# A one-column ordering write moved from VectorE to ScalarE in a fused attention and feed-forward kernel

## The chip, the cores and the metric

The kernel runs on one core of a Trainium2 chip. The core has five engines that run in parallel, each through its own queue in order: TensorE (PE, with its weight loads shown apart as PEld), VectorE (DVE), ScalarE (ACT), GpSimd (POOL) and SyncE (SP, which issues most DMAs). An engine waits for another through semaphores. The metric is the device time in microseconds of one execution, as a median of three runs; lower is better. "Visit 13" below means a turn of the kernel's main loop, explained in the section on the kernel.

## The reference

Attention with normalised queries and keys over 8 batches, 12 heads, 448 positions and a head size of 64, followed by a feed-forward block with SiLU:

```python
def rmsnorm(x, g):
    rms = np.sqrt(np.mean(x * x, axis=-1, keepdims=True) + 1e-06)
    return x / rms * g
q_n, k_n = (rmsnorm(q, g_q), rmsnorm(k, g_k))
scores = scale * np.matmul(q_n, k_n.transpose(0, 1, 3, 2))
attn = np.exp(scores - np.max(scores, axis=-1, keepdims=True))
attn = attn / (np.sum(attn, axis=-1, keepdims=True) + 1e-09)
x = np.matmul(attn, v)               # then (B,H,S,D) -> (B*S, H*D)
h = x @ w_in                         # 3584 x 768 times 768 x 2048
g = h * (1.0 / (1.0 + np.exp(-h)))
out = g @ w_out                      # 2048 x 768
```

All data is fp32.

## The kernel before

The attention part is a loop over 24 visits, `visit(c)` followed by `between(c)`. A visit handles four heads: two pairs `i`, each with two heads `h`. Scores are made with the keys on the partitions, in chunks `j` of 2 x 64 keys; the last, smaller chunk is called `LEFT`. `scores(c, j, i)` (line 590) is four 64x64 matmuls, which fill the four quadrants of the array together and which the trace shows as two groups of four, since each fp32 product takes two passes. ScalarE then takes the exponential of two banks (line 604); its scale is the reciprocal norm of the key rows.

The weighted sums, `weigh(c, j, step)` (line 615), are again 64x64 matmuls. Two PSUM banks, `banks[0]` and `banks[1]` (tile `av`), hold the sums of the two pairs. A matmul reads 64 rows of the array, the upper or the lower half, and which half goes to which bank depends on `step`: in arrangement 0 the half is `i`, in arrangement 1 it is the other one (line 625). So each bank gets sums from both halves over a visit. When the arrangement turns, a matmul of one row half would write a bank which matmuls of the other half may still be writing. Two things keep them in order. `turn(step)` (line 609) writes one unused column of `banks[1]`, column S, from a constant: this write waits for the earlier matmuls into the bank, and the next matmuls into the bank wait for the write. Where the visit is `crowded` (line 1337: those in `visits`, in `sums_visits`, and visits 6, 12 and 18; seven in all) the second turn of the visit makes no write, and `weigh` instead puts a drain into TensorE's queue (line 622), which holds until its earlier matmuls are done. On a turn `weigh` takes bank 1 first.

The order inside a visit is written out by hand (lines 1272 to 1327), and the schedule is manual: each engine's queue holds its instructions in the order of the program text. In a visit the order is: scores (0,0); the squares of the next visit's q (up to visit 6); the last two sums of the visit before in arrangement 0; `turn(1)`; scores (0,1); the last sum in arrangement 1; copies or divisions of the finished sums; scores (1,0) and (1,1); squares of k; sum (0) in arrangement 1; scores (2,0); sum (1) in arrangement 1; `turn(0)`; scores (2,1); sums (0) and (1) in arrangement 0; scores (LEFT). The exponentials of a chunk stand on ScalarE's queue where the scores stand in the text.

The squares (`Norm.squares`, line 398) are a ScalarE activation followed by a VectorE reduction; then come a small VectorE operation (line 430) and a power on GpSimd (line 434). In `before`, `split` (line 1333) runs the two parts of some of these pieces apart: part 0 (the ScalarE square) ahead of the sums and the turn, part 1 (the VectorE reduction and what follows) after the turn. This is done for the first piece of q around `turn(1)` and for the last piece of k around `turn(0)`.

GROUP is 6. In visits 0 to 5 the normalisation of the next visit, the reciprocals of the softmax sums (`invert`, line 680) and the rounding of w_in (`Rounder`, line 55: ScalarE, VectorE and GpSimd) go beside the visits. From visit 6 on, the normalisation is done in `between`, which also fills TensorE with products of the feed-forward's first layer (`fill`, line 1211; class `Seven`), of which the SiLU (line 917) runs on ScalarE. As SiLU and the exponential use different tables of ScalarE, `between` ends with a small exponential (line 1380) that makes the table load happen there. PSUM banks `sc` for the scores are two; transposes of the next q and k use them too. After the loop `visit(24)` does the last sums, and the second layer follows.

Of the kernel before, what the change touches and what calls it, by code (L numbers as in the profile page):

```python
# [12 lines left out]
AF = mybir.ActivationFunctionType  # L13
ALU = mybir.AluOpType
AX = mybir.AxisListType
# [367 lines left out]
class Norm:  # L383
# [11 lines left out]
        n = self.at[0 if j == self.z.KEYS else i][0] + 2 * j + h  # L395
        return self.rms[c % 2][:, n : n + 1]

    def squares(self, rows, t, out, parts=(0, 1)):
        nc, n = self.nc, out.shape[1]
        t = t[0 : rows.shape[0], 0 : rows.shape[1]]  # L400
        if 0 in parts:
            nc.scalar.activation(t, rows, AF.Square)  # L402
        if 1 in parts:
            nc.vector.tensor_reduce(  # L404
                out=out, in_=t.rearrange("p (n d) -> p n d", n=n), axis=AX.X, op=ALU.add
            )

    def squares_q(self, c, rows, t, i, parts=(0, 1)):
        R = self.z.R
        size = self.nq * self.z.D  # L410
        self.squares(rows[0:R, ts(i, size)], t, self.rms[c % 2][0:R, ts(i, self.nq)], parts)

    def squares_k(self, c, rows, t, i, parts=(0, 1)):
        start, n = self.at[i]
        first = (self.z.KA, self.z.KB)[i]
        self.squares(
            rows[:, ds(first, n * self.z.D)], t, self.rms[c % 2][:, ds(start, n)], parts
        )

    def root(self, c, name, i=None):  # L420

# [45 lines left out]
def bounded(  # L467
# [3 lines left out]
    P, D, R, J, S = z.P, z.D, z.R, z.J, z.S  # L471
# [6 lines left out]
    NC, loads, place, norm, spare, ones, first = (  # L478
        own[name] for name in ("NC", "loads", "place", "norm", "spare", "ones", "first")
    )  # L480
    GROUP = z.NPAIR
# [9 lines left out]
    parts = mem.tile([P, 2 * S], F32, name="parts")  # L491
    work = mem.tile([P, 16 * S + z.NK], F32, name="work")
    at = 0

    def piece(n):
        nonlocal at
        at += n
        return work[:, at - n : at]
# [16 lines left out]
    n = 2 * room.COLS  # L515
# [10 lines left out]
    def raw_of(c):  # L526
        return own["second_q"] if c == 1 else raw_q[c % 2]

    def q_of(c):
        return rows_q[c % 2 if c < GROUP else 0]  # L530

    def load_q(c):

        if 0 < c < GROUP:
            loads["q"](c, raw_of(c), True)
        elif GROUP <= c < NC:
            loads["q"](c, q_of(c), False)

    def weights(c, j):

        return other if j == 0 and c < GROUP and c % 2 else e[j]
# [45 lines left out]
    weighed = dict(step=1)  # L587
    banks = [None] * 2

    def scores(c, j, i=None):  # L590


        two = ps.tile([P, 2, BANK], F32, name="sc", bufs=2)
        for half in range(2):
            pair = half if j == LEFT else i
            keys = kT[:, ds((z.KA, z.KB)[0 if j == LEFT else i] + j * P, P)]
            for h in range(2):
                rows = ds(h * D, D)
                nc.tensor.matmul(  # L599
                    two[ds(half * D, D), h, 0:S], keys[rows, ts(half, D)], qT[rows, pair, :],  # L600
                    start=True, stop=True,
                )
        for h in range(2):
            nc.scalar.activation(  # L604
                eleft[:, h] if j == LEFT else weights(c, j)[:, i, h], two[:, h, 0:S], AF.Exp,
                scale=norm.column(c, i, h, j),
            )

    def turn(step, later=False):

        weighed["drain"] = later
        if step != weighed["step"] and not later:
            nc.vector.tensor_copy(banks[1][:, S : S + 1], minus_half)  # L613

    def weigh(c, j, step=0):

        order = (0, 1) if step == weighed["step"] else (1, 0)  # L620
        if step != weighed["step"] and weighed.get("drain"):
            nc.tensor.drain()
        weighed["step"] = step
        for i in order:
            half = i if j == LEFT else (i + step) % 2
            rows = ds(half * D, D)
            if j == 0 and step == 1:
                banks[i] = ps.tile([P, BANK], F32, name=f"av{i}")
                sums[i] = banks[i][:, 0:S]
            for h in range(2):  # L630
                if j == LEFT:
                    v, w = place[f"vleft{c % 2}"][rows, ts(h, D)], eleft[rows, h]
                else:
                    w = weights(c, j)[rows, i, h]
                    if j == LEFT - 1:
                        v = place[f"vlast{c % 2}"][rows, ts(2 * i + h, D)]
                    else:
                        v = place["v"][rows, ds(((2 * i + h) * (LEFT - 1) + j) * D, D)]
                nc.tensor.matmul(  # L639
                    sums[i][ds(h * D, D), :], v, w,  # L640
                    start=(j == 0 and step == 1), stop=(j == LEFT - 1 and step == 1),
                )
# [58 lines left out]
    def normalise(c):  # L701


        if c >= NC:
            return []

        def piece(name, i, parts=(0, 1)):
            t = scratch[i if c < GROUP + 2 else 0]
            source = raw_of(c) if c < GROUP else q_of(c)
            if name == "q":  # L710
                norm.squares_q(c, source, t, i, parts)
            else:
                norm.squares_k(c, place[f"k{c % 2}"], t, i, parts)
            if 1 not in parts:
                return
            if name == "q" and c < GROUP:
                norm.root(c, name, i)
                norm.scale(c, source, q_of(c), i, nc.gpsimd)
                if i == 1 and c + 2 < GROUP:
                    load_q(c + 2)  # L720
            elif i == 1:
                norm.root(c, name)
                if name == "q":
                    for m in range(2):
                        norm.scale(c, source, q_of(c), m, nc.gpsimd)

        return [
            lambda *parts, a=a: piece(*a, *parts)
            for a in (("q", 0), ("q", 1), ("k", 0), ("k", 1))
        ]  # L730


    def minus(a, b, out):
# [257 lines left out]
    size = HF * 2 * P  # L991
# [6 lines left out]
    for at in ((1, 2), (2, 1), (2, 2)):  # L998
        a = take(2 * z.HALF)
        results[at] = [a[:, ts(t, z.HALF)] for t in range(2)]  # L1000
    a = take(2 * z.HALF)
# [250 lines left out]
    visits = {GROUP + 2: "rr", GROUP + 4: "rr"}  # L1252
    sums_halves = {-6: [(0, 0)], -5: [(0, 1)], -4: [(0, 2)], -3: [(0, 3)]}
    sums_halves.update({8: [(3, 0), (3, 1)], 9: [(3, 2), (3, 3)]})
    sums_visits = {GROUP + 1: 1, GROUP + 3: 2}
# [16 lines left out]
    def visit(c):  # L1272

        beside = normalise(c + 1) if c <= GROUP else []
        if c < NC:
            scores(c, 0, 0)
        split(beside[0:1], 0)
        if c > 0:
            weigh(c - 1, LEFT)
            weigh(c - 1, LEFT - 1, 0)  # L1280
            turn(1)
        split(beside[0:1], 1)
        if c < NC:
            scores(c, 0, 1)
        if c == 0:
            run_all(beside[1:2])
        if c > 0:
            weigh(c - 1, LEFT - 1, 1)
            if c - 1 < EARLY:
                for i in range(2):  # L1290
                    nc.vector.tensor_copy(x_of(c - 1, i), sums[i])
                run_all(beside[1:2])
                if inverting:
                    if c > 1:
                        divide(c - 2, None)
                    run_all(inverting)
                    inverting.clear()
            else:
                divide(c - 1, sums)
                run_all(beside[1:2])  # L1300
                if c < NC and c % GROUP == 0:
                    for i in range(0 if c == GROUP else 1, HW):
                        sum_x(last_two(c), i)
                weights_in_visit(c)
            if c + 1 < NC:
                loads["vrest"](c + 1)
        if c == NC:
            return
        scores(c, 1, 0)
        scores(c, 1, 1)  # L1310
        if c < GROUP:
            run_all(beside[2:3])
        weigh(c, 0, 1)
        scores(c, 2, 0)
        if c < GROUP:
            split(beside[3:4], 0)
        weigh(c, 1, 1)
        turn(0, crowded(c))
        if c < GROUP:
            split(beside[3:4], 1)  # L1320
        scores(c, 2, 1)
        weigh(c, 0, 0)
        run_all(add(c, 1))
        weigh(c, 1, 0)
        scores(c, LEFT)
        if c + 1 < NC:
            loads["v"](c + 1)

    def run_all(work):
        for piece in work:  # L1330
            piece()

    def split(work, part):
        for piece in work:
            piece((part,))

    def crowded(c):
        return c in visits or c in sums_visits or (c >= GROUP and c % GROUP == 0)

    def between(c):  # L1340

# [49 lines left out]
    for c in range(NC):  # L1391
        visit(c)
        between(c)
# [9 lines left out]
    for m in range(2):  # L1403
        rows = [staged() for _ in range(2)]
# [215 lines left out]
```

## Time and profile before

| | |
|---|---|
| median of 3 runs | 1348.41 us (1348.09 to 1349.94) |
| profiled execution | 1349.43 us, span of its instructions 1347.6 us |
| granted TensorE clock, mean | 0.997 |
| VectorE idle before the column write, for TensorE | 57.5 us, 27 times |
| exponentials (line 604), 324 of 128x448 | 634 ns each |
| sums (line 639), 1296 matmuls of 64x64 by 448 | 547 ns each, four at a time |
| scores (line 599), 1344 matmuls of 64x64 by 448 | 547 ns each, four at a time |
| ScalarE table load of line 1380, 17 times | 1283 ns each |
| visits 0 to 6 | about 0 to 140 us |
| visits 7 to 23 | about 140 to 757 us |
| second layer and rest | from about 765 us |

The span counts from the first to the last instruction of the profiled execution; the execution's own time is 1.8 us longer. A group of four 64x64 matmuls overlaps with the next one, so that the starts of the groups, and not the length of one matmul, show how fast TensorE goes. Of an instruction that waits, the time line shows in brackets how long its engine was idle before it and which instruction released it.

### The profile page before, as it was taken

Reading aid. Unit: us, or ns where it says so; the run is one execution under the profiler, and the core shown is the slowest. Engines: PE = TensorE matmul, PEld = TensorE weight load, DVE = VectorE, ACT = ScalarE, POOL = GpSimd, SP = SyncE. Lnnn points to the kernel's source line nnn. Section 1 sums busy time; section 2 is a strip of 40 time slices with the busy share of each in tenths; the row PEclk is TensorE's granted clock in tenths of the full one; section 3 lists DMA queues with packets and bytes.
Section 4 is the critical chain, followed back from the end, with each engine's and each line's share of the span. In section 5 each row is a group of like instructions: output and inputs, shape, how many; then the busy total and the mean of one; then the engine's idle time right before and its main releaser. Section 6 shows DMA issues by size and latency. Waiting matters only on the chain.

```text
span 1347.6 us, 19775 instructions
## 1 busy us (share of the span) xinstructions
PE 1315.5 (98%) x7345; PEld 841.3 (62%) x7345; DVE 925.6 (69%) x1634; ACT 515.5 (38%) x884; POOL 343.1 (25%) x241
## 2 busy tenths in 40 slices
PE   8898999999999999999999999999999999999998
PEld 4333444444444444444444455557999999999997
DVE  5687877785655544644544587679878787878785
ACT  7766565655455555545544244320000010101000
POOL 6564534343233332333221044420000000000001
PEclk9999999999999999999999999999999999999999
DMA  9554435333223223222311257521323232322321
GB/s 245 146 143 120 121 111 161 99 99 81 78 76 102 79 78 100 76 75 79 104 54 38 100 171 255 160 98 57 116 74 99 75 98 81 98 89 91 111 62 39
DMA packets 175422, 139.42 MB, mean 103 GB/s; under 512 B 104052, under 2 KB 159284, under 8 KB 175316
## 3 DMA queue, kind: packets, MB, share of 16 engines
q1 hardware_dynamic: 174640, 137.08, 34.5%
q8 instruction: 60, 0.98, 0.3%
q0 software_dynamic: 352, 0.79, 0.2%
q14 instruction: 46, 0.38, 0.1%
q10 hardware_dynamic: 324, 0.20, 0.1%
HBM read 88.47 MB, written 41.29 MB: 96 GB/s over the span
## 4 chain that ended last, share of the span: by engine, by line
PE 84%; DVE 5%; ACT 5%; issue 2%; DMA 2%; SPq 1%; POOL 1%; ACTq 0%; DVEq 0%; POOLq 0%
PE mm L779 27%; PE alone L1086 22%; PE mm L1086 7%; PE alone L779 7%; PE av L639 7%; PE sc L599 7%; PE alone L1123 2%; PE sc L562 1%; ACT work L604 1%; PE sc L580 1%; DVE work L682 1%; PE sc L673 1%; DMA work<-work 1%; PE mm L1123 1%; ACT L1380 1%
## 5 line engine op out<-in xcount | busy, mean ns | idle before, releaser
L779 PE MATMUL mm<-x,W 128*128 128x448 f32 x636 | 253.9, 543 | 3.1 <-DVE stage L737 1.2
L604 ACT ACTIVATE work<-sc,rms 128x448 f32<-128x448 f32 x324 | 184.3, 634 | 83.6 <-PE sc L599 67.1
L434 POOL TENSOR_TENSOR rms<-rms,minus_half 128x14 f32<-128x14 f32 (+4 forms) x55 | 137.9, 2509 | 237.5 <-DVE rms L430 169.2
L779 PEld LDWEIGHTS mm<-x,W 128*128 128x128 f32 x636 | 117.8, 190 | 125.0 <-issue 107.1
L779 PE MATMUL mm<-sums_x,W 128*128 128x448 f32 x456 | 183.0, 542 | 1.2 <-DVE parts L737 1.2
L599 PE MATMUL sc<-work 64*64 64x448 f32 x1344 | 165.1, 547 | 3.1 <-ACT work L604 2.6
L639 PE MATMUL av<-work,rows 64*64 64x448 f32 x1296 | 153.8, 547 | 8.6 <-DVE av L613 7.2
L779 PEld LDWEIGHTS mm<-sums_x,W 128*128 128x128 f32 x456 | 85.3, 190 | 86.9 <-issue 80.8
L653 DVE TENSOR_TENSOR work<-work 128x896 f32<-128x896 f32 (+1 forms) x114 | 124.6, 1126 | 19.7 <-PE av L639 15.1
L461 POOL DMA_DIRECT2D out_dram<-x x4 | 2.3, 566 | 442.9 <-DVE x L737 442.8
L639 PEld LDWEIGHTS av<-work,rows 64*64 64x64 f32 x1296 | 56.1, 133 | 84.1 <-issue 44.3
L599 PEld LDWEIGHTS sc<-work 64*64 64x64 f32 x1344 | 52.0, 133 | 86.5 <-ACT work L604 34.4
L404 DVE TENSOR_REDUCE rms<-squares 112x8 f32<-112x512 f32 (+1 forms) x80 | 52.3, 654 | 64.7 <-ACT squares L402 63.9
L1086 PE MATMUL alone<-W,rows 128*128 128x192 f32 x488 | 92.1, 326 | 0.0
L799 POOL TENSOR_TENSOR parts<-parts,stage 128x448 f32<-128x448 f32 x31 | 42.1, 1357 | 157.5 <-DVE parts L737 157.2
L1086 PEld LDWEIGHTS alone<-W,rows 128*128 128x128 f32 x488 | 81.5, 190 | 0.0
L1086 PE MATMUL alone<-W,work 128*128 128x192 f32 x382 | 72.2, 326 | 0.0
L917 ACT ACTIVATE stage<-stage 128x896 f32<-128x896 f32 x63 | 57.3, 945 | 26.1 <-DVE stage L737 25.4
L1086 PEld LDWEIGHTS alone<-W,work 128*128 128x128 f32 x382 | 63.8, 190 | 0.0
L682 DVE RECIPROCAL work<-sc 128x224 f32<-128x224 f32 x36 | 55.7, 1548 | 11.1 <-PE sc L673 11.1
L1096 ACT COPY squares<-alone 128x192 f32<-128x192 f32 x34 | 10.8, 317 | 137.0 <-PE alone L1086 78.4
L402 ACT ACTIVATE squares<-rows 128x512 f32<-128x512 f32 (+1 forms) x74 | 44.8, 605 | 47.5 <-DVE rms L404 46.0
(249 smaller groups left out, 2124.9 us busy)
## 6 DMA issues: line engine op xcount, KB each, us to landing
hidden<-stage SPq DMA_DIRECT2D x63, 448.0 KB, 2.7
work<-hidden SPq DMA_DIRECT2D x21, 1024.0 KB, 5.0
rows<-in_moe_w_out_dram SPq DMA_DIRECT2D x32, 384.0 KB, 3.4
W<-in_moe_w_in_dram SPq DMA_DIRECT2D x22, 512.0 KB, 5.1
rows<-in_k_dram SPq DMA_DIRECT2D x48, 192.0 KB, 3.2
work<-work SPq DMA_DIRECT2D x144, 56.0 KB, 1.9
rows<-in_q_dram SPq DMA_DIRECT2D x36, 224.0 KB, 3.5
x<-hidden SPq DMA_DIRECT2D x7, 1024.0 KB, 5.7
```

The source lines that it names most:

```text
L402: nc.scalar.activation(t, rows, AF.Square)
L404: nc.vector.tensor_reduce(out=out, in_=t.rearrange("p (n d) -> p n d", n=n), axis=AX.X, op=ALU.add)
L434: nc.gpsimd.tensor_tensor(out=t, in0=t, in1=half, op=ALU.pow)
L599: nc.tensor.matmul(two[ds(half * D, D), h, 0:S], keys[rows, ts(half, D)], qT[rows, pair, :], start=True, stop=True,)
L604: nc.scalar.activation(eleft[:, h] if j == LEFT else weights(c, j)[:, i, h], two[:, h, 0:S], AF.Exp, scale=norm.column(c, i, h, j),)
L639: nc.tensor.matmul(sums[i][ds(h * D, D), :], v, w, start=(j == 0 and step == 1), stop=(j == LEFT - 1 and step == 1),)
L653: nc.vector.tensor_tensor(out=total, in0=total, in1=more, op=ALU.add)
L682: nc.vector.reciprocal(out=r[0][:, rows], in_=t[:, rows])
L779: nc.tensor.matmul(t, self.left(name, s), self.right(name, s), start=s == ends[0], stop=s == ends[1])
L799: nc.gpsimd.tensor_tensor(out=u2, in0=u2, in1=p5, op=ALU.add)
L917: nc.scalar.activation(t, t, AF.Silu)
L1086: nc.tensor.matmul(t, x[:, i], y, start=i == ORDER[0], stop=i == ORDER[-1])
```

## The change

Every turn is now a one-column write by ScalarE; VectorE's writes and the drains are gone, and with them `crowded`. The pieces of squares are no longer split: the first piece of q is issued whole ahead of the sums (its ScalarE square stood there before; its VectorE reduction, the small operation and GpSimd's power and scaling now stand there too), and the last piece of k is issued whole after `turn(0)`, so that its ScalarE square now comes behind the column write, where it came ahead of the sum before.

```diff
-    def turn(step, later=False):
-
-        weighed["drain"] = later
-        if step != weighed["step"] and not later:
-            nc.vector.tensor_copy(banks[1][:, S : S + 1], minus_half)
+    def turn(step):
+
+        if step != weighed["step"]:
+            nc.scalar.copy(banks[1][:, S : S + 1], minus_half)
...
         order = (0, 1) if step == weighed["step"] else (1, 0)
-        if step != weighed["step"] and weighed.get("drain"):
-            nc.tensor.drain()
         weighed["step"] = step
...
         if c < NC:
             scores(c, 0, 0)
-        split(beside[0:1], 0)
+        run_all(beside[0:1])
         if c > 0:
             weigh(c - 1, LEFT)
             weigh(c - 1, LEFT - 1, 0)
             turn(1)
-        split(beside[0:1], 1)
         if c < NC:
             scores(c, 0, 1)
...
         weigh(c, 0, 1)
         scores(c, 2, 0)
+        weigh(c, 1, 1)
+        turn(0)
         if c < GROUP:
-            split(beside[3:4], 0)
-        weigh(c, 1, 1)
-        turn(0, crowded(c))
-        if c < GROUP:
-            split(beside[3:4], 1)
+            run_all(beside[3:4])
         scores(c, 2, 1)
         weigh(c, 0, 0)
         run_all(add(c, 1))
...
-    def split(work, part):
-        for piece in work:
-            piece((part,))
-
-    def crowded(c):
-        return c in visits or c in sums_visits or (c >= GROUP and c % GROUP == 0)
-
```

The rest of the diff removes the `parts` argument from `squares`, `squares_q`, `squares_k` and `normalise`.

## The prediction

> **What bounds the kernel now.** I read the page first (busy shares, slices), then the instructions of the column write and of the drain by source line, then the time line around every one of these 48 places.
>
> ```profile
> PE 1315.5 (98%) x7345; PEld 841.3 (62%) x7345; DVE 925.6 (69%) x1634; ACT 515.5 (38%) x884; POOL 343.1 (25%) x241
> ...
> DVE  5687877785655544644544587679878787878785
> ACT  7766565655455555545544244320000010101000
> ```
>
> TensorE is the bound: 98% busy, so a change is worth what it does to the places where TensorE waits. ScalarE is busy 50 to 70% in the first eight slices (visits 0 to 6, up to some 135 us) and about half after.
>
> ```profile
> L613 DVE COPY av<-minus_half x41: 143/161/164, 17.7 to 761.2; 128x1 f32<-128x1 f32 x41
> ...
>   PEld av L639: 28.7, 41
> ...
>   PE av L639: 10.7, 7
> ```
>
> ```profile
> L622 PEldq DRAIN  x7: 1727/1750/2623, 135.4 to 554.5; - x7
> ```
>
> 41 column writes of 0.16 us on VectorE, and 7 drains. In the waiters' list only 7 column writes hold matmuls up; the rest are done while TensorE still works on the scores in between. The drain's 1.75 us is time in which TensorE works its queue off; what it costs is read from matmul starts. In the steady state a group of four 64x64 matmuls starts every 0.375 us. In visit 7 the last scores group before the drain starts at 173.37 with its last matmul at 173.67, and the next starts at 174.35: about 0.6 us lost. In visit 12 it is 0.3 (345.31 to 346.00, less 0.375).
>
> The largest wait is in visit 2 (time line; start, length, engine, line):
>
> ```profile
> 50.97 1.20 PE L599 MATMUL sc<-work 64*64 64x448 f32 x8
> 51.32 2.96 DVE L682 RECIPROCAL work<-mm 128x224 f32<-128x224 f32 x2
> ...
> 54.20 0.62 DVE L404 TENSOR_REDUCE rms<-squares 128x8 f32<-128x512 f32 x1
> 54.74 0.14 DVE L613 COPY av<-minus_half 128x1 f32<-128x1 f32 x1
> ...
> 54.94 3.23 PE L639 MATMUL av<-work,rows 64*64 64x448 f32 x16 [2.77 <-DVE av L613]
> ...
> 59.27 0.63 ACT L604 ACTIVATE work<-sc,rms 128x448 f32<-128x448 f32 x1 [5.85 <-PE sc L599]
> ```
>
> ```profile
> 40.00:60.00 20.00, 17.23 (x155) 7.17 (x151) 14.74 (x26) 13.53 (x25) 11.40 (x8) 0.91 0.58 170
> ...
> 80.00:100.00 20.00, 20.00 (x167) 8.91 (x169) 17.06 (x27) 16.26 (x29) 12.81 (x8) 1.00 0.61 153
> ```
>
> VectorE is in two reciprocals and a reduction, the column write is queued behind them, and TensorE stands still for 2.77 us. After that 16 matmuls take 3.23 us where 1.7 is usual: the granted clock of that window is 0.91, not 1.00. Then ScalarE has been idle 5.85 us. Visit 3 repeats this (gap 2.75 us before 75.05); visit 1 has 0.84 us before 36.52.
>
> The opposite picture is in the middle, visit 13:
>
> ```profile
> 374.84 0.16 DVE L613 COPY av<-minus_half 128x1 f32<-128x1 f32 x1 [0.42 <-PE av L639]
> 374.91 4.45 ACT L604 ACTIVATE work<-sc,rms 128x448 f32<-128x448 f32 x8
> ...
> 376.11 2.03 PE L599 MATMUL sc<-work 64*64 64x448 f32 x16
> ```
>
> Here VectorE is idle and prompt, and ScalarE is late: its table load and the small activation of L1380 end at 375.01, and eight exponentials follow without a gap. A write on ScalarE stands behind the first two of them.
>
> **What the Trainium skill says.** "ScalarE: Activation LUTs", section "What ACT_TABLE_LOAD costs": an activation with immediate operands takes 186 ns plus 0.833 ns an element, and back-to-back ones overlap by about 93 ns. For one column that is 187 ns. The trace has a near twin:
>
> ```profile
> L1380 ACT ACTIVATE first<-minus_half x17: 202/203/203, 165.5 to 725.7; 128x1 f32<-128x1 f32 x17
> ```
>
> I use 0.20 us, and 0.1 us as what it delays the next instruction (exponentials of 0.63 start every 0.52 here). "TensorE: Matmul & The Clock Gate", section "Part 1: The HAM clock gate": after an idle window of about 3.4 us the clock falls to half. The trace agrees in kind: groups at 0.75 us instead of 0.375 after the wait at 52 to 55 us. "PSUM — Partial Sum Buffer", section "PSUM bank collisions raise a hardware error": different row tiles must not write one bank at once. That is why the wait exists in either form and can't just vanish.
>
> **The change, part by part.** Seven drains go, 41 VectorE writes go, 48 ScalarE writes come: 24 at turn(1) (behind exp(c,0,0), and up to visit 6 behind the square of q too) and 24 at turn(0) (behind exp(c,2,0); up to visit 5 the last square of k comes after it). For each place the new start of the weighted sums is the later of TensorE's natural next start and (ScalarE free, or the last sum ended, + 0.2 + 0.06 us); 0.06 is the latency seen from a column's end to the matmul.
>
> *Visits 0 to 6.* Visit 0: exp(0,2,0) ends at 18.15, so 18.31 instead of 17.95; the square, its reduction and the addition before the next exponential slip with it, +0.3. Visit 1: at turn(1) VectorE's rounding made the write late (29.59); ScalarE is free at 29.40, -0.15. At turn(0) the write is done at 35.58, not 36.47; the additions come 0.65 earlier, scores(1,LEFT) 0.9 earlier, the next exponential about 1.0 earlier: -1.0. Visit 2: turn(1) costs 0.42 (square of q until 46.63), 0.27 of it in VectorE's chain. At turn(0) the write is at 52.2; TensorE no longer waits, and **VectorE is what is late next**: reciprocals until 54.54, two reductions, a small operation until 55.77, addition until 56.8. The exponential at 59.27 comes at 56.9, and as the transposes then run at full clock, visit 3 starts 2.7 earlier: -2.7. Visit 3 is alike, but in visit 4 the copies of the sums stand behind VectorE's second reciprocal, which gains only 1.05: the sums' banks come free late, and -2.3 is left. Visit 4's turn(0) is within that. Visit 5: exp LEFT slips 0.25, but the transposes wait for GpSimd's scaling until 119.06 anyway: 0. Visit 6: the write comes 1.0 earlier, but the division at 133.45 waits for a DMA and holds the banks: 0. Sum -5.85.
>
> *Visits 7 to 23.* In eight of them (10, 12, 13, 14, 17 to 20) the table load makes exp(c,0,0) end after TensorE wants the banks. Visit 13: the write ends at 376.15, sums start at 376.21 instead of 375.31, the next scores 0.85 later; but those after them waited for exponentials before (377.15), so 0.55 is left. ScalarE's exp(1,1) then ends at 380.17, just in time for 380.35. At turn(0) the write ends at 381.48 against a natural 381.47: total 0.57. Five such visits with columns: +2.85. Three had a drain, whose 0.3 goes: +0.25 each, 0.75. The other nine are in time at turn(1). Drains in visits 7, 8, 9: exp ends 173.70, sums at 173.95 for 174.35, so -0.4, -0.47, -0.35: -1.2. Columns at turn(0) in 11, 15, 16, 21, 22, 23: exp(c,2,0) ends about 0.15 after VectorE's write did, +0.1 each; visit 23's turn(1) +0.05: +0.65. Bounds for one write: 0 where TensorE is not ready, 0.17 without the overlap. Sum +3.05. Here TensorE always has filler products behind, so a loss is not taken up later.
>
> *The last visit.*
>
> ```profile
> 760.66 0.62 DVE L734 TENSOR_TENSOR sums_x<-x,sums_x 128x448 f32<-128x448 f32 x1
> ...
> 761.20 0.15 DVE L613 COPY av<-minus_half 128x1 f32<-128x1 f32 x1
> 761.40 0.21 PEld L639 LDWEIGHTS av<-work,rows 64*64 64x64 f32 x8 [2.32 <-DVE av L613]
> 761.41 0.98 PE L639 MATMUL av<-work,rows 64*64 64x448 f32 x8 [1.54 <-DVE av L613]
> ```
>
> ScalarE is free at 760.00: sums at 760.21, end 761.15, the division at 761.28 (VectorE's four sums) instead of 762.46: -1.2. The products of the tail start from it.
>
> VectorE's 41 x 0.16 us of writes are otherwise not on the path; its 57.5 us of waiting in front of them is followed by additions that need the same sums. No DMA is issued at another place in its queue, except that reads of q follow the earlier scaling by the same amounts.
>
> Sum: -5.85 + 3.05 - 1.2 = **-4.0 us**. The profiled execution took 1349.43 (span 1347.6); the median is 1348.41, and I set the difference against that: **1344.4 us**.
>
> **Rivals.**
> 1. *The stalls of visits 1 to 3 are covered by VectorE.* Its busy time is 14 of 20 us there, and the 1.0 to 1.1 us by which its own chain moves may be all: -0.6, -0.8, -0.8 and +0.3 instead of -5.85. Then -1.9 + 3.05 - 1.2 = 0: 1348.4. Against it: ScalarE's 5.85 us idle ended with a scores group at half clock, not with VectorE.
> 2. *ScalarE becomes the bound.* Place: turn(1) in the eight late visits. If the exponentials carry the whole delay through (0.9 us each, 7.2) and each of the 17 writes at turn(0) costs 0.17 (2.9), less drains and tail (2.4), +7.7; with half the early gain (-2.9) it is +4.8: 1353.2. It decides when exp(1,1) ends later than the second group of weigh(1,1) can start; I worked out 0.18 us to spare, so it is near.
> 3. *More early gain.* Half-clock groups vanish and visit 4 follows fully: -8, and +1 less in the middle: 1341.
>
> **Chances.** Forecast 0.45 (1342.5 to 1346.5), rival 1 0.23, rival 2 0.20, rival 3 0.12. The measurement tells 0.2%, 2.7 us, from no change. Faster: 0.12 and most of 0.45, 0.50; same 0.27; slower 0.23. The range takes in rivals 1 and 3 and part of 2: 1341.5 to 1351.
>
> **What would show it.** The waits of 2.77, 2.75 and 1.54 us gone, granted clock 1.00 from 40 to 80 us, visit 7 starting some 6 us earlier; then 3 us lost up to 755, with "PE av <- ACT av" waits of about 0.9 us in the eight visits. Wrong would be: exponentials in visits 2 and 3 still idle for 5 us, or a loss of 0.9 a visit at all visits.

## The result, and the profile after

| | before | after |
|---|---|---|
| median, same sessions | 1349.84 us (12 runs, 1348.09 to 1352.08) | 1347.47 us (12 runs, 1346.43 to 1349.07) |
| ratio, 95% interval | | 0.9984 (0.9975 to 0.9993) |
| profiled execution | 1349.43 us, span 1347.6 | 1347.41 us, span 1345.6 |

The changed kernel is faster by 2.2 us, with an interval of about 0.9 to 3.4 us; the forecast was 4.0. The sign holds, the size is about half, and at 0.16% it lies below the 0.2% that the prediction took as the smallest change to be told from none. (The runs of the kernel before now have a median 1.4 us above that of the first three, so the ratio is the fair comparison; the two profiled executions differ by 2.0 us.)

The page of the kernel after: busy time of each engine, then the slices of VectorE and ScalarE.

```profile
PE 1312.5 (98%) x7345; PEld 848.1 (63%) x7345; DVE 915.4 (68%) x1593; ACT 519.6 (39%) x932; POOL 346.3 (26%) x241
...
DVE  5787776785645444644544586789878787878785
ACT  7866565655445455545544244320000000101000
```

VectorE has 41 instructions less, ScalarE 48 more, and TensorE the same 7345 matmuls. The busy shares hardly move, so nothing of the result can be read from them. The instructions of the column write, with the waiters behind it (us, times):

```profile
L608 ACT COPY av<-minus_half x48: 158/171/234, 17.6 to 758.8; 128x1 f32<-128x1 f32 x48
...
  PE av L632: 9.6, 13
```

The write itself costs 0.17 us against VectorE's 0.16. It now holds up matmuls at 13 places instead of 7 (10.7 us before). The total is nearly the same, but the places are others: the waits of 2.77 and 2.75 us are gone and the one of 1.54 is 0.28, while the eight visits with the table load came in with 0.69 to 1.29 us each. (A wait of 1.66 us at turn(1) of visit 1 hardly changed, to 1.36.)

The time line at the largest wait of before, visit 2:

```profile
50.41 2.95 DVE L675 RECIPROCAL work<-mm 128x224 f32<-128x224 f32 x2
51.18 0.20 ACT L608 COPY av<-minus_half 128x1 f32<-128x1 f32 x1
...
51.44 1.73 PE L632 MATMUL av<-work,rows 64*64 64x448 f32 x16
...
54.47 2.10 DVE L646 TENSOR_TENSOR work<-work 128x896 f32<-128x896 f32 x2
55.67 1.16 ACT L600 ACTIVATE work<-sc,rms 128x448 f32<-128x448 f32 x2 [2.80 <-DVE work L646]
```

The write stands beside the two reciprocals instead of behind them; 16 sums take 1.73 us where they took 3.23, and ScalarE's idle time before the next exponential is 2.80 us, ended by VectorE's addition, where it was 5.85, ended by scores at half clock. The same stretches as before, in the view of windows:

```profile
40.00:60.00 20.00, 18.63 (x181) 7.61 (x183) 14.01 (x22) 15.96 (x31) 13.75 (x9) 1.00 0.60 173
60.00:80.00 20.00, 18.55 (x169) 7.51 (x165) 16.32 (x25) 15.48 (x30) 12.73 (x7) 1.00 0.50 134
80.00:100.00 20.00, 17.55 (x153) 7.21 (x145) 17.10 (x26) 14.02 (x26) 12.45 (x7) 1.00 0.69 182
```

The granted clock from 40 to 60 us is 1.00 where it was 0.91, and so from 60 to 80. But from 80 to 100 us TensorE is busy 17.55 us where it was 20.00: here some of the gain is lost again (the stretches don't hold quite the same work any more).

Both kernels issue the same matmuls in the same order, so their starts can be compared one by one. The first scores of a visit show how far the kernel is ahead, and the difference of two neighbours is what the visit changed. Visit 7, for instance, starts at 165.40 us before (the 140 us given above are where visit 6's own sums end) and 5.46 us earlier after. In us, negative is faster:

| part | forecast | measured |
|---|---|---|
| visits 0 to 2 | -3.55 | -3.63 (+0.14, -0.89, -2.88) |
| visits 3 and 4 | -2.3 | -1.29 (-2.88, +1.59) |
| visits 5 and 6 | 0 | -0.21 |
| visits 7, 8, 9, drains gone | -1.22 | -0.21 (-0.38, +0.45, -0.28) |
| visits 13, 14, 17, 19, late columns | +2.28 (0.57 each) | +3.22 (0.80, 0.85, 0.78, 0.79) |
| visits 10, 12, 18, late, drains gone | +0.75 (0.25 each) | +1.33 (0.45, 0.45, 0.43) |
| visit 20, late | +0.57 | -0.49 |
| visits 11, 15, 16, 21, 22 | +0.5 | 0 |
| visit 23 and the last | -1.05 | -0.81 |
| ahead of visit 0, and behind the last matmul of the loop | 0 | +0.07 (-0.34, +0.41) |
| sum | -4.02 | -2.02 |

The time line of visit 13, in the middle:

```profile
371.19 0.17 ACT L608 COPY av<-minus_half 128x1 f32<-128x1 f32 x1
...
371.41 0.98 PE L632 MATMUL av<-work,rows 64*64 64x448 f32 x8 [0.69 <-ACT av L608]
...
373.21 3.50 ACT L600 ACTIVATE work<-sc,rms 128x448 f32<-128x448 f32 x6 [0.78 <-PE sc L595]
...
375.23 1.20 PE L632 MATMUL av<-work,rows 64*64 64x448 f32 x8
```

and eight matmuls of the same program text, weigh(13,1,1), in the kernel before:

```profile
379.46 0.93 PE L639 MATMUL av<-work,rows 64*64 64x448 f32 x8
```

The wait at the write is as forecast: the sums start 0.87 us later in the visit than before, for which 0.90 was forecast. The new thing is in the last line: the eight sums take 1.20 us where they took 0.93. Three matmuls of the first group start between 375.23 and 375.27, and the fourth, which reads the second half of exp(13,1,1), at 375.47, after that exponential has ended at 375.42. Seen alone this is 0.24 us. But the quadrant that came late stays late in the groups that follow: in the last scores of the visit it is still 0.16 us behind the other three, and what comes after the visit starts by it.

### The profile page after: what moved, and what is told of

Read it like the earlier page. It is cut to its first block, busy times and chain, and to the rows that moved or that the text cites. A ratio compares the mean times of both kernels' runs of the same rounds, so it can differ in the third digit from the quotient of the medians.

```text
span 1345.6 us, 19745 instructions
## 1 busy us (share of the span) xinstructions
PE 1312.5 (98%) x7345; PEld 848.1 (63%) x7345; DVE 915.4 (68%) x1593; ACT 519.6 (39%) x932; POOL 346.3 (26%) x241
## 4 chain that ended last, share of the span: by engine, by line
PE 83%; DVE 5%; ACT 5%; DMA 3%; issue 2%; SPq 1%; POOL 0%; ACTq 0%; DVEq 0%; POOLq 0%
PE mm L767 25%; PE alone L1074 22%; PE mm L1074 7%; PE av L632 7%; PE alone L767 7%; PE sc L595 7%; PE alone L1111 2%; DVE work L675 1%; PE sc L558 1%; DMA work<-work 1%; PE sc L576 1%; DMA hidden<-stage 1%; PE sc L666 1%; ACT work L600 1%; ACT L1358 1%
## 5 line engine op out<-in xcount | busy, mean ns | idle before, releaser
L430 POOL TENSOR_TENSOR rms<-rms,minus_half 128x14 f32<-128x14 f32 (+4 forms) x55 | 140.9, 2563 | 236.5 <-DVE rms L426 187.0
L632 PEld LDWEIGHTS av<-work,rows 64*64 64x64 f32 x1296 | 59.3, 132 | 86.3 <-issue 34.2
L595 PEld LDWEIGHTS sc<-work 64*64 64x64 f32 x1344 | 56.0, 132 | 75.8 <-issue 25.9
```

Of the source, the lines that this page charges most:

```text
L430: nc.gpsimd.tensor_tensor(out=t, in0=t, in1=half, op=ALU.pow)
L595: nc.tensor.matmul(two[ds(half * D, D), h, 0:S], keys[rows, ts(half, D)], qT[rows, pair, :], start=True, stop=True,)
L632: nc.tensor.matmul(sums[i][ds(h * D, D), :], v, w, start=(j == 0 and step == 1), stop=(j == LEFT - 1 and step == 1),)
```

## The experiments

Each kernel is measured against the kernel before in its own session. "Ahead" is worked out from matmul starts, as above.

**1. The late visits: is it ScalarE's queue there?** From the changed kernel, only turn(1) of the eight late visits goes back to VectorE.

```diff
-    def turn(step):
+    def turn(step, c):
...
-            nc.scalar.copy(banks[1][:, S : S + 1], minus_half)
+            on_vector = step == 1 and c in (10, 12, 13, 14, 17, 18, 19, 20)
+            copy_one = nc.vector.tensor_copy if on_vector else nc.scalar.copy
+            copy_one(banks[1][:, S : S + 1], minus_half)
...
```

> The changed kernel with turn(1) of visits 10, 12, 13, 14 and 17 to 20 back on VectorE, all other writes on ScalarE. Theory (in these visits the write stands behind two late exponentials, and one of the four matmuls of the first group of weigh(c,1,1) then waits for exp(c,1,1)): each of the eight visits loses nothing at turn(1), so about 0.8 us a visit comes back: 5.5 to 6.5 us less than the changed kernel, 1341.0 to 1342.5 us, ratio to before about 0.994. Rival (the 0.8 us come from turn(0) or from ScalarE's longer queue as a whole): less than 2 us comes back.

Measured: 1342.75 us against 1350.17, ratio 0.9941 (0.9928 to 0.9955), the forecast ratio. The line of the write, by source:

```profile
L610 DVE COPY av<-minus_half x8: 155/161/163, 267.4 to 615.9; 128x1 f32<-128x1 f32 x8
```

Eight writes of 0.16 us, moved, are worth some 5 us (4.8 by the table below without visit 20): that is the queue in front of them and not the instruction. By visit, together with the next experiment:

| visit | forecast | after | 1: on VectorE | 2: ahead of the exponentials |
|---|---|---|---|---|
| 13 | +0.57 | +0.80 | +0.09 | +0.19 |
| 14 | +0.57 | +0.85 | +0.11 | +0.19 |
| 17 | +0.57 | +0.78 | +0.07 | +0.18 |
| 19 | +0.57 | +0.79 | +0.03 | +0.13 |
| 10 | +0.25 | +0.45 | 0 | +0.09 |
| 12 | +0.25 | +0.45 | -0.27 | -0.18 |
| 18 | +0.25 | +0.43 | -0.30 | -0.20 |
| 20 | +0.57 | -0.49 | -1.22 | -1.12 |

**2. The engine or the place in its queue?** The write stays on ScalarE everywhere. In the eight visits the two exponentials of scores(c,0,0) are issued behind turn(1) instead of ahead of it; the part of the edit left out here makes `scores` put them into the list `held`.

```diff
...
+        held = []
...
-            scores(c, 0, 0)
+            scores(c, 0, 0, held if c in (10, 12, 13, 14, 17, 18, 19, 20) else None)
...
             turn(1)
+        run_all(held)
```

> The changed kernel with the two exponentials of scores (c,0,0) put behind the write of turn(1) in ScalarE's queue in visits 10, 12, 13, 14 and 17 to 20; the write stays on ScalarE. Theory (the place in the queue costs, not the engine): the write comes right after the small activation of the table load, TensorE is not held, and about 0.6 to 0.8 us a visit comes back, 4.5 to 6 us in all: 1341.5 to 1343 us. Rival (ScalarE takes longer to write and to release than VectorE): under 2 us comes back, and 'PE av waits for ACT av' stays in the eight visits.

Measured: 1342.48 us against 1350.17, ratio 0.994 (0.9926 to 0.9954). The time line of visit 13:

```profile
370.28 0.15 ACT L614 COPY av<-minus_half 128x1 f32<-128x1 f32 x1
370.36 4.47 ACT L601 ACTIVATE work<-sc,rms 128x448 f32<-128x448 f32 x8
...
370.66 0.93 PE L638 MATMUL av<-work,rows 64*64 64x448 f32 x8
...
374.92 0.93 PE L638 MATMUL av<-work,rows 64*64 64x448 f32 x8
```

The write follows the small activation directly, nothing waits for it here (0.17 to 0.27 us in visits 10, 12 and 18), the exponentials run on without a gap (4.47 us for eight, as before the change), and the sums of weigh(13,1,1) take 0.93 us again. So it is the place in the queue, not the engine, and the split quadrants go with the lateness. The 0.1 us between the last two columns of the table is about what one write in front of the exponentials delays them by.

**3. The early visits alone.** From the kernel before, turn(0) of visits 1, 2 and 3 alone goes to ScalarE.

```diff
...
-            nc.vector.tensor_copy(banks[1][:, S : S + 1], minus_half)
+            copy_one = nc.scalar.copy if step == 0 and c in (1, 2, 3) else nc.vector.tensor_copy
+            copy_one(banks[1][:, S : S + 1], minus_half)
...
```

> The kernel before with only three writes moved to ScalarE, turn(0) of visits 1, 2 and 3; drains, splits and all else as before. Theory (the early gain is those three stalls and the half clock after them): by the start of visit 4 about 6 us are gained, in visit 4 about 1.5 us of it go back, and 4.5 to 5.5 us stay to the end: ratio 0.9960 to 0.9967. Rival (VectorE's own chain covers the stalls, the early gain of the changed kernel came from the other 45 writes): under 2 us.

Measured: 1347.65 us against 1350.17, ratio 0.9979 (0.997 to 0.9987), less than expected. Visits 1, 2 and 3 bring -0.52, -3.05 and -3.03, which is the early gain in full. Visit 4 gives back +2.51 where about 1.5 was expected: its turn(1) is still VectorE's here, and TensorE waits 2.47 us for a write that stands behind a division (which itself waits for DMAs), rounding and two reciprocals. In the profiled execution it is still 3.91 ahead at the end of the loop and only 0.47 at the end of the program. The time line and the window at the end of the loop:

```profile
757.50 0.98 PE L640 MATMUL av<-work,rows 64*64 64x448 f32 x8 [1.54 <-DVE av L614]
758.55 1.16 DVE L698 TENSOR_TENSOR x<-av,work 128x448 f32<-128x448 f32 x2 [1.10 <-PE av L640]
759.85 7.80 PE L780 MATMUL alone<-x,W 128*128 128x448 f32 x12 [1.37 <-DVE x L698]
```

```profile
755.00:775.00 20.00, 17.09 (x52) 7.81 (x45) 9.83 (x20) 3.77 (x7) 0.00 (x0) 0.83 0.28 97
```

Twelve products take 7.80 us here; the kernel of experiment 6 below does ten in 4.00. The granted clock of the window is 0.83, and 1.00 in the kernel before. Eight groups ran at 0.75 us instead of 0.375, which is 3.05 us in all. The kernel before has the same two waits (1.54 and 1.37) without this, so it comes on in some executions and not in others; the last section says which. The median execution need not have it, so the missing gain is explained in visit 4, and after the loop for the profiled execution alone.

**4. What takes back visit 4's gain?** In the changed kernel the time line of VectorE and of the waiting sums there reads:

```profile
78.16 1.16 DVE L690 TENSOR_TENSOR x<-x,work 128x448 f32<-128x448 f32 x2 [1.95 <-DMA work<-work]
79.23 1.55 DVE L675 RECIPROCAL work<-mm 128x224 f32<-128x224 f32 x1
...
83.04 1.54 DVE L675 RECIPROCAL work<-mm 128x224 f32<-128x224 f32 x1
...
85.25 1.15 DVE L1278 COPY x<-av 128x448 f32<-128x448 f32 x2
...
85.92 1.12 PE L632 MATMUL av<-work,rows 64*64 64x448 f32 x6 [1.28 <-DVE x L1278]
```

The second of the reciprocals that run in visit 3 ended at 70.60. SP issued the six DMAs that spread the result over the partitions between 70.62 and 75.86, and VectorE's division waited until 78.16 for them, idle for 1.95 us. Then come a reciprocal, rounding, a second reciprocal and a reduction, and only then the copies that free the sums' banks: TensorE waits 1.28 us. In this experiment the later of the two (at 83.04) goes behind the copies.

```diff
+                if c == GROUP // 2 + 1:
+                    run_all(second)
...
         if c == GROUP // 2:
+            second.append(prompt.pop())
...
```

> The changed kernel with the second half of the reciprocals of visit 3, and the spreading DMAs that follow it, moved from before visit 4 to behind visit 4's copies of the sums. Theory (in visit 4 the gain goes back because the copies that free the sums' banks stand on VectorE behind a reciprocal chain that waited for the spreading DMAs): the 1.28 us wait of TensorE before weigh(4,0,1) goes and visit 4 loses under 0.5 us against the kernel before instead of 1.59; part of it may come back as a later division in visit 4 or 5. Rival (TensorE is held in visit 4 by ScalarE or by DMA loads of q and k): visit 4 loses 1.4 us or more as before.

Measured: 1346.77 us against 1349.78, ratio 0.9974 (0.9962 to 0.9985). The time line at the same place:

```profile
85.33 1.14 DVE L1278 COPY x<-av 128x448 f32<-128x448 f32 x2
86.00 1.13 PE L632 MATMUL av<-work,rows 64*64 64x448 f32 x6
...
87.19 1.55 DVE L675 RECIPROCAL work<-mm 128x224 f32<-128x224 f32 x1
```

The sums follow with no wait shown, and visit 4 loses +0.28 instead of +1.59. That the copies stand behind too much in VectorE's queue is shown. The share of the DMAs in it is only read from the trace: VectorE still waits 1.67 us for them in this experiment, and taking one reciprocal of 1.55 us out of the way was enough. The rest of the time doesn't follow to its full size: in this execution the first groups of scores in visit 0 start 0.75 to 0.80 us apart, as at half clock, where they start 0.43 apart in the changed kernel, which costs 0.79 us, and the interval overlaps that of the changed kernel. What visit 4 is worth in the whole time isn't resolved.

**5. The drains alone.** From the kernel before, each drain becomes a write by ScalarE, and VectorE's other 41 writes stay.

```diff
-        weighed["drain"] = later
-        if step != weighed["step"] and not later:
-            nc.vector.tensor_copy(banks[1][:, S : S + 1], minus_half)
+        if step != weighed["step"]:
+            copy_one = nc.scalar.copy if later else nc.vector.tensor_copy
+            copy_one(banks[1][:, S : S + 1], minus_half)
...
-        if step != weighed["step"] and weighed.get("drain"):
-            nc.tensor.drain()
```

> The kernel before with the seven drains replaced by ScalarE writes at the same place; all else as before. Theory: visits 7 and 9 gain 0.3 to 0.4 us, visits 10, 12 and 18 about 0.3, visit 8 gains 0.5 at the turn and gives it back in the products after it (VectorE's rounding and the stores that follow set its end), visit 6 gains nothing: 1.3 to 1.9 us in all up to visit 23. Rival (a drain's 1.75 us are lost TensorE time): 7 us or more.

Measured: 1350.35 us against 1349.78, ratio 1.0 (0.9991 to 1.0008): nothing. At the turns themselves the gain is there: the first matmul behind comes 0.54, 0.56 and 0.51 us earlier in visits 7, 8 and 9, and 0.28 in visit 10. By the end of the visit it is -0.38, +1.31, -0.36 and -0.01, and -0.27 and -0.30 in visits 12 and 18; these six sum to zero, because of visit 8.

That 0.54 becomes 0.38 in visit 7 is again a matter of quadrants. In the kernel before, the fourth one is already 0.28 us late ahead of the turn, and behind the drain all four start within 0.02 us. Behind the write it is still 0.23 us late, and what follows the visit starts by it.

The time line of visit 8 in this kernel:

```profile
222.22 0.53 ACT L795 COPY stage<-mm 128x448 f32<-128x448 f32 x1 [5.55 <-DMA hidden<-stage]
...
227.34 2.52 PE L777 MATMUL mm<-sums_x,W 128*128 128x448 f32 x6 [2.02 <-DVE parts L735]
```

and in the changed kernel, with the issue of the store on SP's queue:

```profile
211.82 1.61 SPq L800 DMA_DIRECT2D hidden<-stage  x2
```

```profile
217.14 0.53 ACT L785 COPY stage<-mm 128x448 f32<-128x448 f32 x1 [4.69 <-DMA hidden<-stage]
```

ScalarE waits some 5 us for the store of the stage it wants to overwrite, and TensorE waits for what VectorE does behind ScalarE's copy. Against the kernel before, the copy comes +0.45 us later in the visit in the changed kernel, +1.31 in this one and -0.15 in the first one of experiment 7, and the visit's end moves by +0.45, +1.31 and -0.15: the copy sets it. The store is issued 17.52 us into the visit before, and 17.68, 17.78 and 17.26 us in these three, so that most of the difference is when it lands. In the changed kernel the gain of 0.38 us is thus there up to that product, and 0.83 is lost at it. The loss doesn't belong to the drain's removal as such, for the first kernel of experiment 7 has no drain either and ends the visit 0.15 us earlier than the kernel before; the runs don't explain its size.

The profile of this kernel also shows how much one execution can differ: visit 3, whose code is that of the kernel before, is 1.69 us shorter, and visit 4 0.70 longer (see the last section).

**6. The last visit alone.** From the kernel before, only the write of visit 24 goes to ScalarE.

```diff
...
-            nc.vector.tensor_copy(banks[1][:, S : S + 1], minus_half)
+            copy_one = nc.scalar.copy if c == NC else nc.vector.tensor_copy
+            copy_one(banks[1][:, S : S + 1], minus_half)
...
-            turn(1)
+            turn(1, False, c)
...
```

> The kernel before with one write moved: turn(1) of visit 24 on ScalarE. Theory: the products after the loop start 0.8 to 1.3 us earlier in a profile and the rest keeps its length, save that fewer executions find TensorE at half clock there (3 us each): the median 1 to 2 us below before. Rival (the division waits for VectorE's four sums anyway): under 0.3 us.

Measured: 1348.1 us against 1349.78, ratio 0.9984 (0.9976 to 0.9992), as forecast. The time line:

```profile
759.83 0.16 ACT L614 COPY av<-minus_half 128x1 f32<-128x1 f32 x1
...
760.04 0.98 PE L640 MATMUL av<-work,rows 64*64 64x448 f32 x8 [0.28 <-ACT av L614]
...
761.09 1.16 DVE L698 TENSOR_TENSOR x<-av,work 128x448 f32<-128x448 f32 x2
...
762.39 4.00 PE L780 MATMUL alone<-x,W 128*128 128x448 f32 x10 [1.37 <-DVE x L698]
```

By the visit's own clock the products of the second layer start 1.26 us earlier. The wait of 1.54 is 0.28 now. That fewer executions run at half clock there, as the text above expects, is not shown. One write of 48 has the same ratio as the whole change: everything else in it nearly cancels (at the end of the loop the profile of the changed kernel is 2.40 us ahead, and this one 1.36).

**7. Each write on the engine that is free there.** Two versions from the changed kernel. The first has VectorE for turn(1) of visits 7 to 23 and for turn(0) where the kernel before had a column after visit 6; the line that decides is this:

```diff
+            on_vector = step == 1 and 6 < c < NC or step == 0 and c > 6 and not (c in visits or c in sums_visits or c % GROUP == 0)
```

> ScalarE writes in visits 0 to 6, at turn(0) of the crowded visits and in visit 24; VectorE at turn(1) of visits 7 to 23 and at turn(0) of those not crowded; no drains. If the pieces add up: -5.1 us early, -1.5 to -2 from the drains, -0.8 at the end: 7 to 8 us less than before, 1341 to 1342.5 us, ratio 0.9940 to 0.9948. If the drains' gain is given back in each crowded visit as in visit 8: 6 us, ratio 0.9955.

Measured: 1343.75 us against 1350.17, ratio 0.9949 (0.9936 to 0.9963). The loop ends 7.16 us ahead in the profile, but the median lies above what was expected. It is not better than experiments 1 and 2: that turn(0) of the middle visits is on one engine or the other is worth nothing in visits 11, 15, 16, 21 and 22, as the zeros in the first table say, and at most 0.1 us in visits 13, 14, 17 and 19 (-0.01 to +0.02 in this profile, +0.03 to +0.11 in that of experiment 1).

The second adds the later reciprocal of experiment 4 and gives VectorE also the one write of visit 0 and turn(1) of visits 2 and 3:

```diff
+            on_vector = c == 0 or step == 1 and c in (2, 3) or step == 1 and 6 < c < NC or step == 0 and c > 6 and not (c in visits or c in sums_visits or c % GROUP == 0)
```

> ScalarE writes at turn(0) of visits 1 to 6, at turn(1) of visits 1 and 4 to 6, at turn(0) of the crowded visits and in visit 24; VectorE writes in visit 0, at turn(1) of visits 2, 3 and 7 to 23 and at turn(0) of the visits not crowded; no drains; the second reciprocal of visit 3 behind visit 4's copies. If the pieces add up as the profiles of the single ones show: -6.5 us by visit 5, -1.3 from the drains, -1.2 at the end, 8 to 9 us less than before: 1340.5 to 1342 us, ratio 0.9933 to 0.9941. If VectorE's place in visits 2 and 3 costs again what ScalarE's did: 0.8 us less gain, ratio about 0.9945.

Measured: 1343.03 us against 1350.33, ratio 0.9947 (0.9934 to 0.9961). That misses its forecast, and is no gain over the others. The profiled execution lost 0.79 us in visit 0 at half clock, as in experiment 4, and 0.83 in visit 8. Visit 4 gives back only +0.65. But turn(1) in visits 2 and 3 now costs +1.41 each, where ScalarE's write cost +0.39 and +0.42: the reduction of q is no longer split around the turn, and on VectorE it stands ahead of the write. By the end of each visit 0.3 us of this is left (-2.58 and -2.59 against -2.88 twice). The split belonged to VectorE's write; without it, ScalarE's is the right one there.

The intervals of experiments 1, 2 and 7 overlap. The plainest of them is experiment 2: ScalarE's write at every turn, with two exponentials moved behind it in eight visits, at 0.994 of the kernel before and so better than both kernels.

## Why the prediction was half right

By the first table, the 2.0 us between forecast and profile are three losses that were put too low (the late visits by 1.5 us, visits 3 and 4 by 1.0, visits 7 to 9 by 1.0), less 1.1 us of chance in visit 20 and 0.5 us that turn(0) did not cost.

**What bounds the kernel, and what the write costs: right.** The write costs 0.17 us, nowhere more than 0.23, and its effect is that of the queue in front of it (experiments 1 and 2). One reading is wrong, though nothing in the sum rests on it: a slice of the page is 33.7 us, so that visits 0 to 6 up to 135 us are its first four slices, with ScalarE busy 60 to 80%, and not the first eight.

**Visits 0 to 2: right**, -3.63 for -3.55. In visit 2 the exponential starts at 55.67; the visit began 1.08 us earlier, so this is 56.75 on the clock of before, for which 56.9 was forecast. VectorE is what is late next there, as was said. Rival 1, that VectorE covers the stalls, falls: ScalarE's idle time fell by 3 us, and experiment 3 has -3.05 and -3.03 from these writes alone.

**Visits 3 and 4: mis-sized**, -1.29 for -2.3. The step saw that "the copies of the sums stand behind VectorE's second reciprocal, which gains only 1.05". It put too little on that queue: visit 4 starts 6.84 us earlier and the copies only 5.00, and TensorE waits 1.28 us for them. Experiment 4 shows that the queue in front of the copies is the cause. That the six DMAs ahead of the division are what holds the queue up (VectorE idles 1.95 us for them) is read from the trace and not tested.

**The late visits: the step that failed.** "ScalarE's exp(1,1) then ends at 380.17, just in time for 380.35 … total 0.57". Up to there the working holds. In visit 13, 0.53 us of the delay are left ahead of weigh(1,1), for which 0.55 was forecast; on the clock of before the exponential ends at 380.18; and the second group of weigh(1,1) starts 0.19 us after it, for which 0.18 was forecast. What failed is that only the second group was taken to need this exponential. All four matmuls of the first group are issued together, and one of them reads its second half. That one came 0.24 us late and its quadrant stayed late, which made 0.80 of 0.57 and, together with the drain's worth there, 0.45 of 0.25. Over seven visits this is 4.55 us instead of 3.03, the largest part of the miss. Experiments 1 and 2 take the lateness away, and the split goes with it. Rival 2 had named the place, but not what happened there: its point, an exponential later than the second group, was not reached, the exponentials don't carry the whole 0.9 us through, and turn(0) costs at most 0.1 us and not 0.17.

**Drains in visits 7, 8 and 9: right in 7 and 9, wrong at the end of visit 8.** Visits 7 and 9 have -0.38 and -0.28 for -0.4 and -0.35. In visit 8 the landing of a store sets the end, and "-0.47" became +0.45. I had taken it that filler products always let a gain through; where the filler waits for a stage to come free, it doesn't.

**Columns at turn(0) in visits 11, 15, 16, 21 and 22: cost 0**, not 0.1 each; the write is hidden behind scores that run anyway. **The last visit: right**, -1.26 for -1.2 by experiment 6. Visit 23 lost some 0.45 (-0.81 + 1.26) where +0.15 was forecast for its two writes: ScalarE's write at turn(1) ended at 725.38 and the sums started at 725.44, where they could have at 725.04.

**Visit 20 proves nothing.** It changed by -0.49, -1.22, +0.61, -1.12, +0.80, +0.60 and +0.49 in the profiles of the changed kernel and of the kernels of experiments 1, 3, 2, 7 (first), 5 and 7 (second). Experiments 3 and 5 left the code of this visit as it was before. ScalarE waits there for a store to land, and between these executions this came 0.2 to 2.3 us after the visit's start. That it helped the changed kernel by 1.06 us against its forecast is chance.

Left open: what decides when the stores in visits 8 and 20 land, whether earlier DMAs would free visit 4, and what experiment 2 with the later reciprocal would give, which was not tried.

## What to carry to other kernels

The price of a small ordering instruction is what stands ahead of it in its engine's queue, so choose its engine and its place in the queue for each spot, and not one engine for all. Where a stall goes, follow what the next waiting engine is fed by, DMAs included, to the end of the chain: more than half of visit 3's gain was taken back in visit 4. And where several matmuls are issued together, look at the operand of each of them, not at the group's first.

## What the runs showed of the hardware

- **Quadrants that fall out of step stay so.** One of four 64x64 matmuls that came 0.24 us late made eight sums take 1.20 instead of 0.93 us, and in the changed kernel the eight scores after them also take 1.20 in the time line. A one-column write narrows the split and doesn't end it (0.29 to 0.20 us at visit 13's turn(0)); a drain does (0.28 to 0.02 us in visit 7 of the kernel before).
- **Whether a wait halves the clock depends on where it falls.** In the clock records of all ten traces, every change of the granted clock lies on a grid of 3.413 us that runs on through the execution, and a half clock inside the kernel lasts one or two steps of it. A step in which TensorE idled 2.16 us or more by the trace was always followed by half clock; a step at full clock with 2.00 us or less never was (one at half clock with 0.67 us was). Visit 3 has the same code and the same wait of 2.75 us in the kernel before and in the kernel of experiment 5. Two neighbouring steps of the grid in each (kernel before first; the clock is the third number from the right):

```profile
72.10:75.51 3.41, 0.67 (x9) 0.24 (x12) 3.38 (x6) 1.47 (x4) 1.94 (x2) 1.00 0.00 1
75.51:78.92 3.41, 3.41 (x24) 1.00 (x16) 2.58 (x4) 0.00 (x0) 2.58 (x1) 0.50 0.30 73
```

```profile
73.04:76.45 3.41, 1.67 (x20) 0.78 (x24) 2.92 (x6) 0.24 (x1) 1.80 (x2) 1.00 0.14 34
76.45:79.87 3.42, 3.42 (x35) 1.72 (x27) 3.35 (x6) 2.48 (x5) 2.15 (x2) 1.00 0.30 70
```

In the first the wait falls into one step, of which TensorE is busy 0.67 us, and half clock follows; in the second it falls into two, and none follows. So too at the end of the loop: the waits of 1.54 and 1.37 us fall into two steps in the kernel before, with 1.54 and 1.37 us idle, and 2.24 us of them into one in experiment 3, where half clock then costs 3.05 us. The Trainium skill, "TensorE: Matmul & The Clock Gate", section "Part 1: The HAM clock gate", has the monitor's window running freely, whatever the kernel does, and gives about 3.4 us for an idle window. The grid agrees with both; but a window need not be idle as a whole, 2.16 us of it were enough here.
- **Executions of one kernel spread with the clock.** Of 29 of the kernel before in one session, the 5 with a mean granted clock of 0.998 took 1348.9 us on average, the 17 with 0.997 1350.0, and the 7 with less 1351.2. All 12 of the changed kernel had 0.998 or 0.999.
- **A drain of 1.75 us in the trace costs 0.3 to 0.4 us more than a write.** When it was replaced, visits 7, 9, 12 and 18 gained 0.27 to 0.38 us by their end; in visit 10 the 0.28 us of the turn was lost again later. The rest of the 1.75 us is work that TensorE had to do anyway.
